# Decay products in one rounded form, one tile for a pair's turned exponentials, a sixth attention output, and another order of the work

## The chip, the cores and the metric

The kernel runs on one core of one Trainium2 chip. The metric is the time of one execution on the device in microseconds (us). A profile is one execution taken by the hardware profiler.

## The reference

Three stages on a batch of 4, 576 tokens, 8 heads of 64, all in float32:

```python
# 1. attention with a running decay, per batch and head
scores = scale * q @ k.T;  cum = cumsum(log(clip(f, 1e-4, 1)))
scores = where(causal, -1e9, scores + cum[:, None] - cum[None, :])
attn = exp(scores - max);  attn /= attn.sum() + 1e-9
x = attn @ v                                   # heads side by side: 576 x 512
# 2. gated feed-forward with a convolution over three tokens
h = relu(x @ w_in)                             # 512 -> 1024
x = (h * sigmoid(conv3(h, conv_w))) @ w_out    # 1024 -> 512
# 3. real part of a 2-D Fourier transform, layer norm, feed-forward
u = x + real(fft(fft(x, axis=tokens), axis=channels))
un = (u - mean(u)) / sqrt(var(u) + 1e-6)
out = u + relu(un @ w_ch1) @ w_ch2             # 512 -> 2048 -> 512
```

## The kernel before, in words

**Attention** goes by pairs of heads, 16 pairs. One tile `qk` holds q and k of both heads, one head in rows 0 to 63 and the other in rows 64 to 127. `score` makes the scores of a pair: for each block of 128 queries (`i` from 0 to 4) a product of q and k in fp32 over the keys up to the diagonal, and onto it, in the same PSUM bank, the decay, as a second product of a column that picks the head (`sel`) with rows that hold -8 times the running sum (`cum`). `cum` is float32 rounded to the form that the array takes in one pass (fp32r), so it is held in two parts, the rounded rows and what the rounding left, and a decay product has 64 rows: 0 to 63 for one head, 64 to 127 for the other. The blocks come as `TX`, block 4 in two halves with blocks 1 and 0, and `TY`, blocks 3 and 2; TX's ranges share banks, (4, first half) with 1 and (4, second half) with 0. There are `NS` = 4 banks for scores. VectorE adds the causal mask, keeps the minimum of each row (scores carry a minus sign) and writes to SBUF; ScalarE takes the exponential and its sum. `trans` turns the exponentials in blocks of 128 by TensorE, and `evac` copies them from PSUM into a tile `pt`, one for even and one for odd heads, on VectorE and ScalarE. `pv` multiplies with v for both heads, scales by the reciprocal sums into `xr`, and splits the result on ScalarE (rounded) and GpSimd (the rest) into a slot of `xs`, a ring of `NX` = 5.

**Pair 0** begins from nothing: `f` lands in `ft`, VectorE and ScalarE take the logarithm and the running sum in two halves and make `cum` from it. For the first of pair 0's groups of ranges (`SELF` = 1) the decay isn't taken from `cum`, but from `ft` itself in fp32, 32 rows, with a column of -8 in the head's row that comes behind f in the same tile. Its four products are issued together behind the four of q and k. Ahead of all that, `NWARM` = 4 matmuls of zeros, which nobody reads, occupy TensorE.

**The second stage**, for each batch of four pairs, is `bc_chunks`: eight chunks of x @ w_in (each matmul reads one slot of `xs`), the convolution and the gate, and then eight of the product with `w_out`. They are put between the steps of later pairs. The weights are unpacked from a 64-bit form by ScalarE, GpSimd and VectorE (`decode`). The third stage follows from about 380 us on: the transforms, and the last feed-forward.

**The order** is the kernel's own: operations are recorded in program order, and `Plan.order` places them by a list scheduler. `cost_of` gives the duration of each, `forward` places them on five queues, `backward` gives due times, both `ROUNDS` times over; a string of letters, `SHIFT`, then shifts each operation's due time. `lead` and `hold` make an operation due earlier, or keep it from a time before which it is not to start. What `together` records is emitted without anything between. Each engine then runs its queue in that order and waits for data by semaphores. Nearly all instructions thus have the line of two helpers: L596 for those recorded together, L607 for the others; they are told apart by their tiles: `att_qk` q and k, `att_t__67` and `att_t__66` `cum` and `sel`, `att_rb__68` `ft` at the start, `att_pt` the turned exponentials, `bc_xs` the attention outputs, `wprep` the weights on their way.

## Time and profile before

| | |
|---|---|
| median of 3 runs | 839.71 us (839.46 to 839.72) |
| the profiled execution's own time | 843.63 us |
| its span, first to last instruction | 841.9 us |
| TensorE busy | 820.2 us, 97% |
| VectorE, ScalarE, GpSimd busy | 640.0, 428.8, 243.8 us |

Busy times are sums over the whole span; the three stages have different fill. A fp32 matmul stands in the trace as two rows of one instruction each, a rounded one as one row; the ends of matmuls are modelled, so the distance from one start to the next says more than a row's own length. The column PEclk tells the clock that the throttle granted as a share of 2.4 GHz, where the profile recorded it.

### The profile page before, as it was taken

The page shows a single profiled execution, that of the slowest core. Times are in us where ns is not written, and L with a number is a line of the kernel's source. Part 1 is how long each engine was busy: PE and PEld are TensorE (multiplying, and loading weights), DVE is VectorE, ACT ScalarE, POOL GpSimd, SP SyncE. Part 2 cuts the span into 40 slices and gives each one's busy share as a digit, 9 for nine tenths or more (in the row PEclk, how much of TensorE's full clock was granted, in tenths as well). Part 3 has the DMA queues.
Part 4 walks back from the last instruction along what each step waited for, and adds up shares of the span by engine and source line. Part 5 has one row for each costly group of instructions (what it writes and reads, how often), then busy time and mean ns, then how long its engine had stood idle before and what let it go on. Part 6 is the DMA issues. An engine that isn't in the chain of part 4 may idle for free.

```text
span 841.9 us, 15293 instructions
## 1 busy us (share of the span) xinstructions
PE 820.2 (97%) x5392; PEld 706.0 (84%) x5392; DVE 640.0 (76%) x1598; ACT 428.8 (51%) x1053; POOL 243.8 (29%) x279
## 2 busy tenths in 40 slices
PE   9999999999999999998999999999999999999998
PEld 5667778699888988898888888888888889888886
DVE  6988899965996694159577979769778698967574
ACT  5987889843874673265344354335423452313120
POOL 1243445410361134177546460222012210000000
PEclk9999999999999999999999999999999999999999
DMA  6555456789248727785986844533646326241222
GB/s 203 170 163 168 152 177 213 221 290 284 105 132 258 245 83 231 256 259 164 251 240 161 195 145 121 168 114 93 207 142 160 125 76 187 52 151 38 80 72 87
DMA packets 98124, 139.67 MB, mean 166 GB/s; under 512 B 17076, under 2 KB 60116, under 8 KB 98048
## 3 DMA queue, kind: packets, MB, share of 16 engines
...
q0 software_dynamic: 576, 2.95, 1.1%
q8 instruction: 42, 0.69, 0.3%
q14 instruction: 34, 0.28, 0.1%
HBM read 105.78 MB, written 35.04 MB: 167 GB/s over the span
## 4 chain that ended last, share of the span: by engine, by line
PE 84%; DVE 7%; ACT 4%; DMA 2%; issue 1%; POOL 1%; SPq 0%; DVEq 0%; ACTq 0%; POOLq 0%
PE psc_c__4736 L607 11%; PE psc_c__4735 L607 11%; PE psbc_bc__549 L607 10%; PE psbc_bc__548 L607 10%; PE psdft_x__3965 L607 5%; PE psdft_x__3966 L607 5%; PE psatt_s__169 L596 4%; PE psc_c__4864 L607 4%; PE psc_c__4863 L607 4%; PE psc_c__4861 L607 4%; PE psc_c__4862 L607 4%; PE psatt_s__167 L596 3%; PE psatt_u__166 L607 2%; PE psatt_u__171 L596 2%; PE psatt_u__166 L596 2%; PE psatt_u__171 L607 2%
## 5 line engine op out<-in xcount | busy, mean ns | idle before, releaser
L607 ACT ACTIVATE bc_xs__131<-ml_t__5420 128x320 fp32r<-128x320 f32 (+1 forms) x78 | 34.9, 450 | 104.9 <-DVE ml_t__5420 L607 88.2
L607 PE MATMUL psbc_bc__548<-bc_xs__131,bc_wi__130 128*128 128x288 f32 x384 | 67.4, 303 | 1.1 <-ACT glu_t__138 L607 1.0
L607 PE MATMUL psbc_bc__549<-bc_xs__131,bc_wi__130 128*128 128x288 f32 x384 | 68.0, 304 | 0.1
L607 DVE TENSOR_TENSOR ml_t__5420<-psc_c__4736,ml_t__5420 128x320 f32<-128x320 f32 (+1 forms) x91 | 40.9, 462 | 23.6 <-PE psc_c__4736 L607 19.4
L607 DVE TENSOR_TENSOR ml_t__5420<-psc_c__4735,ml_t__5420 128x320 f32<-128x320 f32 (+1 forms) x91 | 40.9, 460 | 21.6 <-PE psc_c__4735 L607 20.0
L607 PEld LDWEIGHTS psbc_bc__548<-bc_xs__131,bc_wi__130 128*128 128x128 f32 x384 | 55.1, 188 | 2.6 <-ACT glu_t__138 L607 1.3
L607 PEld LDWEIGHTS psbc_bc__549<-bc_xs__131,bc_wi__130 128*128 128x128 f32 x384 | 55.2, 188 | 1.9 <-issue 0.7
L607 DVE SCALAR_TENSOR_TENSOR bc_xs__131<-ml_t__5420,bc_xs__131 128x320 fp32r<-128x320 f32 (+1 forms) x78 | 39.3, 508 | 15.0 <-ACT bc_xs__131 L607 13.5
L607 POOL TENSOR_SCALAR wprep_dw__125<-wprep_dw__125 128x512 f32<-128x512 f32 x24 | 16.4, 683 | 110.7 <-ACT wprep_dw__125 L607 110.7
L607 POOL TENSOR_SCALAR wprep_dw__122<-wprep_dw__122 128x512 f32<-128x512 f32 x24 | 16.6, 691 | 83.0 <-ACT wprep_dw__122 L607 83.0
L607 DVE SCALAR_TENSOR_TENSOR glu_cv__157<-glu_t__138,bc_cw__132,glu_cv__157 128x576 f32<-128x576 f32 x32 | 32.4, 1013 | 7.2 <-ACT glu_cv__157 L607 6.9
L607 DVE SCALAR_TENSOR_TENSOR glu_cv__158<-glu_t__139,bc_cw__132,glu_cv__158 128x576 f32<-128x576 f32 x32 | 31.4, 981 | 4.1 <-ACT glu_cv__158 L607 3.9
L607 DVE COPY glu_t__140<-psbc_bc__549 128x256 f32<-128x256 f32 (+2 forms) x48 | 9.9, 261 | 30.4 <-PE psbc_bc__549 L607 27.9
L607 ACT ACTIVATE ml_t__5422<-ml_t__5420 128x320 fp32r<-128x320 f32 (+1 forms) x26 | 11.5, 448 | 41.3 <-DVE ml_t__5420 L607 34.5
L607 ACT ACTIVATE glu_t__140<-psbc_bc__548 128x256 f32<-128x256 f32 (+2 forms) x48 | 8.6, 251 | 36.5 <-PE psbc_bc__548 L607 31.1
L596 PE MATMUL psatt_u__171<-att_pt__101,att_tv__92 128*64 128x448 f32 (+3 forms) x80 | 21.6, 417 | 1.0 <-ACT att_pt__102 L607 1.0
L596 PE MATMUL psatt_u__171<-att_pt__102,att_tv__93 128*64 128x448 f32 (+3 forms) x80 | 21.6, 417 | 0.0
L607 POOL TENSOR_TENSOR bc_xs__131<-att_xr__69,bc_xs__131 128x576 fp32r<-128x576 f32 x8 | 12.7, 1585 | 26.4 <-ACT bc_xs__131 L607 26.4
L607 ACT ACTIVATE wprep_dw__125<-wprep_dr__124 128x512 f32<-128x512 f32 x24 | 15.9, 663 | 8.6 <-DMA wprep_dr__124<-in_moe_w_ch_dram 4.1
L596 PE MATMUL psatt_u__166<-att_pt__102,att_tv__100 128*64 128x448 f32 (+4 forms) x72 | 19.3, 413 | 0.0
L596 PE MATMUL psatt_u__166<-att_pt__101,att_tv__99 128*64 128x448 f32 (+4 forms) x72 | 19.3, 413 | 0.0
L607 DVE SCALAR_TENSOR_TENSOR glu_cv__158<-glu_cv__158,glu_t__139 128x576 f32<-128x576 f32 x16 | 15.0, 936 | 4.9 <-ACT glu_cv__158 L607 4.9
(899 smaller groups left out, 2958.9 us busy)
## 6 DMA issues: line engine op xcount, KB each, us to landing
wprep_dr__124<-in_moe_w_ch_dram SPq DMA_DIRECT2D x16, 512.0 KB
...
bc_wo__133<-dram_t__328 SPq DMA_DIRECT2D x13, 512.0 KB
...
```

The lines of the kernel that those rows point to most:

```text
L596: getattr(eng[op.eng], f)(**{k: v.real() if isinstance(v, View) else v for k, v in kw.items()})
L607: getattr(eng[op.eng], op.fn)(**kw)
```

## The change

The decay products of all pairs take the rounded rows `cum`; the fp32 form, its column in the tile of f and the input that held it go. In pair 0 each range's products of q and k, and each range's decay products, are recorded as a group of their own; in the other pairs a group now has q-k and decay of one range before those of the next, and each range begins with a start flag of its own. The turned exponentials of a pair lie in one tile of 3840 columns instead of two of 2688: the odd head's blocks run backwards in the gaps of the even head's. The ring of attention outputs gets a sixth slot, in another pool. There are six warm-up matmuls instead of four. The later half of w_in may start at 20 us in the plan instead of 30, w_out at 50 instead of 60. The planner prices a group by its columns and the number of its matmuls, and its model of the clock has two levels of activity. `SHIFT` is another string, and there are 58 rounds instead of 27.

```diff
--- before.py
+++ after.py
@@ -21,14 +21,14 @@
 NZT, NZR, NPQ, NUN, NUS = 1, 1, 0, 2, 1
 NZS = 1
 G3 = 6
-NCV, NZZ, NZO, NX = 2, 4, 2, 5
-NUO, NWARM = 1, 4
+NCV, NZZ, NZO, NX = 2, 4, 2, 6
+NUO, NWARM = 1, 6
 LASTW = 256
 NTV = 4
-NPT = 1
-DRAIN = 120.0
-XW, H_IN, H_OUT, H_CH = 6, 3e4, 6e4, 0.0
-NS, NU, NSPLIT, SELF = 4, 2, 4, 1
+NPT, NXR, NRT = 1, 2, 2
+DRAIN = 200.0
+XW, H_IN0, H_IN, H_OUT, H_CH = 6, 0.0, 20000.0, 50000.0, 0.0
+NS, NU, NSPLIT = 4, 2, 4
 LINE = 64
 NPB = 2
 BK3 = (3,)
@@ -37,81 +37,81 @@
 NFO = DFF // 128
 NFC = DCH // 128
 HALF = S // 2
-ROUNDS = 27
+ROUNDS = 58
 LETTERS = "ABCDEFGHIJKLMNOPQRSTUVWXYZabcdefghijklmnopqrstuvwxyz0123456789+-"
 SHIFT = """
...
 """
 KW = [64 + 128 * i for i in range(5)]
-PTW, QW = 2688, S + 64
+QW = S + 64
 QK = QW + S
 UW, ZW = DM + 2, 640
 HL = ((0, 0), (1, 0), (0, 1))
@@ -293,7 +293,8 @@
 
 def cost_of(eng, fn, kw, subs=None):
     if subs:
-        return DRAIN + sum(cost_of(eng, f, k) for f, k in subs) / 2
+        one = [k["out"].free() / 2.4 * (2.0 if k["rhs"].dtype == F32 else 1.0) for _, k in subs]
+        return sum(one) + 10.0 * len(subs)
     o = kw["out"]
     src = kw.get("in_", kw.get("in0", kw.get("data0", o)))
     n = float(prod(o.shape[1:]))
@@ -505,14 +506,16 @@
 
     def forward(self, prio):
         ops, busy = self.ops, {}
-        wire, port = [0.0], [-1e9, -1e9]
+        wire, port, cold = [0.0], [-1e9, -1e9], [True]
 
         def place(i, t):
             o = ops[i]
             o.took = o.cost
             if o.eng == "PE":
                 tick = int(t // 3413.3)
-                if busy.get(tick - 1, 0) < 2500:
+                while len(cold) <= tick:
+                    cold.append(busy.get(len(cold) - 1, 0) < (3060 if cold[-1] else 2500))
+                if cold[tick]:
                     o.took = 2 * o.cost - 12.0
                 busy[tick] = busy.get(tick, 0) + o.work
             if o.pair:
@@ -701,8 +704,8 @@
             heads[2 * p + x] = dict(t=t[64 * x:64 * x + 64])
 
     plan.lead = 2 * LEAD
-    ft = att.tile([128, S + NH], F32, tag="rb")
-    one = att.tile([128, S], F32, tag="xr", bufs=2)
+    ft = att.tile([128, S], F32, tag="rb")
+    one = att.tile([128, S], F32, tag="xr", bufs=NXR)
     one, ft = one[0:NH], ft[0:NH]
     V.memset(out=one, value=1.0)
     dma(out=ft, in_=f)
@@ -725,7 +728,8 @@
     A.activation(out=sel, in_=mask[:, S:S + NH], func=AF.Copy)
 
     wi = bc.tile([128, 2, 4, DFF], F32R, tag="wi")
-    xs = bc.tile([128, NX, 2, S], F32R, tag="xs")
+    xs = bc.tile([128, 5, 2, S], F32R, tag="xs")
+    xs = [xs[:, i] for i in range(5)] + [ga.tile([128, 2, S], F32R) for _ in range(NX - 5)]
     cw = bc.tile([128, 3 * NFO], F32, tag="cw")
 
     def load_conv():
@@ -778,7 +782,9 @@
         Pt.append(row)
     sums = {}
     if NWARM:
+        plan.lead = 3 * LEAD
         V.memset(out=Pt[1][4][:, 0:256], value=0.0)
+        plan.lead = 0.0
         ps = ps_att.tile([128, 512], F32, tag="u", bufs=NU)
         for i in range(NWARM):
             mm(ps[:, 0:256], Pt[1][4][:, 0:128], Pt[1][4][:, 0:256], True, True)
@@ -794,42 +800,38 @@
     TX = (((4, 0, HALF), (1, 0, KW[1])), ((4, HALF, S), (0, 0, KW[0])))
     TY = (((3, 0, KW[3]),), ((2, 0, KW[2]),))
 
-    TXY = TX + TY
-
     def score(p, tiles):
         two = (2 * p, 2 * p + 1)
         if tiles[0] is TX[0]:
             sums[p] = att.tile([128, 2, 5], F32, tag="sum", bufs=2)
             for n in two:
                 heads[n]["nb"] = att.tile([128, 6], F32, tag="nb", bufs=4)
-        subs, picks, todo = [], [], []
+        subs, todo = [], []
         for items in tiles:
-            ps = [ps_att.tile([128, 512], F32, tag="s", bufs=NS) for _ in two]
-            col = 0
+            ps = None
             for i, c0, c1 in items:
                 w = KW[i]
-                if col and p == 0 and items is TX[0]:
-                    plan.together("PE", picks)
-                    ps, col, picks = [ps_att.tile([128, 512], F32, tag="s", bufs=NS) for _ in two], 0, []
+                if ps is None or p == 0 and items is TX[0]:
+                    ps, col = [ps_att.tile([128, 512], F32, tag="s", bufs=NS) for _ in two], 0
                 o = [z[:, col:col + c1 - c0] for z in ps]
                 for n in two:
                     t = heads[n]["t"]
                     subs.append(("matmul", dict(out=o[n % 2], lhsT=t[:, w - 64:w + 64], rhs=t[:, QW + c0:QW + c1],
-                                                start=col == 0, stop=False)))
+                                                start=True, stop=False)))
                 if p == 0:
                     plan.together("PE", subs)
                     subs = []
                 for n in two:
                     r = slice(64 * (n % 2), 64 * (n % 2) + 64)
-                    if p == 0 and items in TXY[:SELF]:
-                        one_of, row = ft[:, S + n:S + n + 1].over(0, [0, 128]), ft[:, c0:c1]
-                    else:
-                        one_of, row = sel[r].over(n, [0, 128]), cum[r, c0:c1]
-                    picks.append(("matmul", dict(out=o[n % 2], lhsT=one_of, rhs=row, start=False,
-                                                 stop=p == 0 and items is TX[0] or (i, c0, c1) == items[-1])))
+                    subs.append(("matmul", dict(out=o[n % 2], lhsT=sel[r].over(n, [0, 128]), rhs=cum[r, c0:c1],
+                                                start=False, stop=True)))
+                if p == 0:
+                    plan.together("PE", subs)
+                    subs = []
                 todo.append((i, c0, c1, o))
                 col += c1 - c0
-        plan.together("PE", subs + picks)
+        if subs:
+            plan.together("PE", subs)
         for i, c0, c1, o in sorted(todo, key=lambda x: (-x[0], x[1])):
             w = KW[i]
             for n in two:
@@ -848,17 +850,18 @@
         r = att.tile([128, 2, 5], F32, tag="r", bufs=2)
         V.tensor_scalar(out=r, in0=sums[p], scalar1=1e-9, scalar2=None, op0=ALU.add)
         V.reciprocal(out=r, in_=r)
-        rt = att.tile([10, 128], F32, tag="rt", bufs=2)
+        rt = att.tile([10, 128], F32, tag="rt", bufs=NRT)
         ps = ps_att.tile([128, 512], F32, tag="u", bufs=NU)
         transpose(ps[0:10, 0:128], r.over(0, [1, 10]))
         A.activation(out=rt, in_=ps[0:10, 0:128], func=AF.Copy)
         dma(out=Flat(r_d, 1280 * p, [128, 10], [1, 128]), in_=rt)
 
     def pt_hi(n, j, q, *dims):
-        return heads[n]["pt"].over(64 + 512 * j + q, *dims)
-
-    def evac(n, src, j, q, nb, step, eng):
-        h_ = pt_hi(n, j, q, [step, nb], [1, 128])
+        return heads[n]["pt"].over(3264 - 640 * j + q if n % 2 else 64 + 512 * j + q, *dims)
+
+    def evac(n, src, j, q, nb, eng, far=False):
+        step = (2560, -2048) if far else (512, -640)
+        h_ = pt_hi(n, j, q, [step[n % 2], nb], [1, 128])
         if eng is V:
             V.tensor_copy(out=h_, in_=src.group(nb))
         else:
@@ -866,7 +869,7 @@
 
     def trans(n, grp):
         if grp == 4:
-            heads[n]["pt"] = att.tile([128, PTW], F32, tag=f"pt{n % 2}", bufs=NPT)
+            heads[n]["pt"] = heads[n - 1]["pt"] if n % 2 else att.tile([128, 3840], F32, tag="pt", bufs=NPT)
         P = Pt[n % (2 * NPB)]
         ps = ps_att.tile([128, 512], F32, tag="u", bufs=NU)
 
@@ -879,32 +882,32 @@
 
         if grp == 4:
             full(4, 0)
-            evac(n, ps, 0, 448, 4, 512, V)
+            evac(n, ps, 0, 448, 4, V)
         elif grp == 3:
             full(3, 0)
             diag(3, 384)
-            evac(n, ps, 0, 320, 4, 512, A)
+            evac(n, ps, 0, 320, 4, A)
         elif grp == 2:
             full(2, 0)
             diag(2, 256)
-            evac(n, ps[:, 0:384], 0, 192, 3, 512, A)
+            evac(n, ps[:, 0:384], 0, 192, 3, A)
         else:
             full(1, 0)
             diag(1, 128)
             diag(0, 256)
             diag(4, 384)
-            evac(n, ps[:, 0:256], 0, 64, 2, 512, A)
-            evac(n, ps[:, 256:512], 0, -64, 2, 2560, V)
+            evac(n, ps[:, 0:256], 0, 64, 2, A)
+            evac(n, ps[:, 256:512], 0, -64, 2, V, True)
 
     xhl = {}
     xrb = {}
 
     def pv(p):
         two = (2 * p, 2 * p + 1)
-        rb = att.tile([128, S + NH], F32, tag="rb")
+        rb = att.tile([128, S], F32, tag="rb")
         for x in range(2):
-            dma(out=rb[64 * x:64 * x + 64, 0:S], in_=Flat(r_d, 1280 * p + 640 * x + 64, [0, 64], [1, S]))
-        xr = att.tile([128, S], F32, tag="xr", bufs=2)
+            dma(out=rb[64 * x:64 * x + 64], in_=Flat(r_d, 1280 * p + 640 * x + 64, [0, 64], [1, S]))
+        xr = att.tile([128, S], F32, tag="xr", bufs=NXR)
         subs, todo = [], []
         for q0, q1, js in ((128, S, (0, 2, 3, 4, 1)), (0, 128, (0,))):
             ps = ps_att.tile([128, 512], F32, tag="u", bufs=NU)
@@ -920,7 +923,7 @@
             V.tensor_tensor(out=xr[:, q0:q1], in0=ps[:, 0:q1 - q0], in1=rb[:, q0:q1], op=ALU.mult)
         for n in two:
             del heads[n]
-        xh, xl = xs[:, p % NX, 0], xs[:, p % NX, 1]
+        xh, xl = xs[p % NX][:, 0], xs[p % NX][:, 1]
         hi(xh, xr)
         lo(G, xl, xr, xh)
         xhl[p] = (xh, xl)
@@ -1013,7 +1016,7 @@
 
     prep = {}
     for k in range(8):
-        prep.setdefault(k // 2, []).append((load_w_in, 2 * k if k < 4 else 2 * k - 7, H_IN if k > 3 else 0.0))
+        prep.setdefault(k // 2, []).append((load_w_in, 2 * k if k < 4 else 2 * k - 7, H_IN if k > 3 else H_IN0))
         prep.setdefault(XW + k // 2, []).append((load_w_out, k, H_OUT))
     prep[0].append((lambda u: load_conv(), 0, 2e4))
     clear_pads()
@@ -1545,8 +1548,7 @@
         order += [b * S + t for t in [0] + list(range(257, 320))]
     c = lambda a: np.ascontiguousarray(a, dtype=np.float32)
     mask = np.concatenate([mask, np.tile(np.eye(NH), (4, 1))], axis=1)
-    pick = -8.0 * np.eye(NH)
-    return {"mask": c(mask), "pick": c(pick), "ident": c(np.eye(128)), "sgn": c(sgn), "dd": c(dd), "ds": c(ds)}, order
+    return {"mask": c(mask), "ident": c(np.eye(128)), "sgn": c(sgn), "dd": c(dd), "ds": c(ds)}, order
 
 
 def kernel(**inputs):
@@ -1568,7 +1570,7 @@
     data = [
         ("qk", qk),
         ("v", vp.reshape(B, H, 5, 128, D).transpose(0, 1, 3, 2, 4)),
-        ("f", np.concatenate([x["f"].reshape(NH, S), consts["pick"]], axis=1)),
+        ("f", x["f"].reshape(NH, S)),
         ("moe_w_in", bits(x["moe_w_in"])),
         ("moe_conv_w", bits(x["moe_conv_w"].reshape(3, NFO, 128).transpose(2, 1, 0).reshape(128, 3 * NFO))),
         ("moe_w_out", bits(x["moe_w_out"])),
```

## Rows read from the trace of the kernel before

**Rows 1.** The page: busy time, share of the span and instructions of each engine.
```profile
PE 820.2 (97%) x5392; PEld 706.0 (84%) x5392; DVE 640.0 (76%) x1598; ACT 428.8 (51%) x1053; POOL 243.8 (29%) x279
```

**Rows 2.** Windows: stretch and length in us, busy us per engine, clock, DMA, GB/s.
```profile
0.00:20.00 20.00, 17.93 (x69) 11.43 (x71) 12.35 (x45) 10.55 (x30) 2.51 (x25) 1.00 0.60 197
20.00:100.00 80.00, 74.04 (x594) 54.11 (x591) 69.23 (x235) 68.03 (x198) 31.60 (x30) 1.00 0.53 166
100.00:430.00 330.00, 321.14 (x2486) 287.08 (x2484) 240.37 (x571) 202.12 (x520) 131.93 (x128) 1.00 0.68 211
430.00:842.00 412.00, 407.06 (x2252) 353.43 (x2250) 318.02 (x751) 148.07 (x308) 77.80 (x97) 1.00 0.45 128
...
150.00:170.00 20.00, 18.08 (x143) 11.85 (x142) 17.96 (x60) 17.19 (x55) 7.16 (x6) 1.00 0.78 232
```

**Rows 3.** Timeline of TensorE, 4 to 19 us: start, length, instruction, idle before.
```profile
5.91 1.22 PE L607 MATMUL psatt_u__166<-att_t__80 128*128 128x256 f32 x2
...
7.41 0.69 PE L596 MATMUL psatt_s__169<-att_qk__70 64*128 64x192 f32 x1 [0.28 <-DMA att_qk__70<-in_qk_dram]
...
8.36 1.32 PE L596 MATMUL psatt_s__167<-att_rb__68 32*128 32x288 f32 x2
9.47 1.16 PE L596 MATMUL psatt_s__168<-att_rb__68 32*128 32x288 f32 x2
...
11.85 0.84 PE L596 MATMUL psatt_s__167<-att_qk__70 64*128 64x288 f32 x1
...
12.49 0.68 PE L596 MATMUL psatt_s__167<-att_qk__70 64*128 64x288 f32 x1
...
13.26 0.58 PE L596 MATMUL psatt_s__167<-att_t__67,att_t__66 64*128 64x288 f32 x1
13.26 0.58 PE L596 MATMUL psatt_s__168<-att_t__67,att_t__66 64*128 64x288 f32 x1
13.64 0.25 PE L596 MATMUL psatt_s__167<-att_t__67,att_t__66 64*128 64x64 f32 x1
...
18.40 0.40 PE L596 MATMUL psatt_s__169<-att_qk__91 64*128 64x288 f32 x1
```

**Rows 4.** Timeline of VectorE, 2 to 14 us.
```profile
4.77 0.91 DVE L607 SCALAR_TENSOR_TENSOR att_t__67<-att_rb__68,att_t__67 32x288 fp32r<-32x288 f32 x2 [0.51 <-ACT att_t__67 L607]
...
7.05 0.91 DVE L607 SCALAR_TENSOR_TENSOR att_t__67<-att_rb__68,att_t__67 32x288 fp32r<-32x288 f32 x2 [0.51 <-ACT att_t__67 L607]
10.68 0.46 DVE L607 CUSTOM_DVE_ANT_0 att_t__80<-psatt_s__168,att_t__65 128x288 f32<-128x288 f32 x1 [2.71 <-PE psatt_s__168 L596]
...
11.06 0.45 DVE L607 CUSTOM_DVE_ANT_0 att_t__75<-psatt_s__167,att_t__65 128x288 f32<-128x288 f32 x1
```

**Rows 5.** Timeline of TensorE, 21 to 27 us.
```profile
21.09 0.64 PE L596 MATMUL psatt_s__169<-att_qk__91 64*128 64x448 f32 x1
...
22.25 0.28 PE L607 MATMUL psatt_u__171<-const_t__61,att_r__97 128*10 128x128 f32 x1
...
23.47 0.53 PE L596 MATMUL psatt_s__167<-att_qk__91 64*128 64x320 f32 x1
...
25.38 0.44 PE L607 MATMUL psatt_u__171<-const_t__61,att_t__77 128*128 128x128 f32 x2
```

**Rows 6.** One tile each: copies from PSUM, ns min/median/max, starts, forms.
```profile
L607 DVE COPY att_pt__101<-psatt_u__166 x16: 408/551/694, 18.2 to 313.5; 128x512 f32<-128x512 f32 x8, 128x256 f32<-128x256 f32 x8
L607 DVE COPY glu_t__140<-psbc_bc__549 x48: 172/181/425, 171.8 to 430.6; 128x256 f32<-128x256 f32 x16, 128x31 f32<-128x31 f32 x16, 128x32 f32<-128x32 f32 x16
```

**Rows 7.** Timeline of TensorE at 108 us and of ScalarE at 133 us.
```profile
108.28 0.59 PE L596 MATMUL psatt_u__166<-att_pt__101,att_tv__99 128*64 128x448 f32 x1
...
133.42 0.67 ACT L607 ACTIVATE bc_xs__131<-att_xr__69 128x576 fp32r<-128x576 f32 x1
```

**Rows 8.** Groups by form, VectorE, 20 to 100 us: count, busy us, mean ns.
```profile
L607 DVE SCALAR_TENSOR_TENSOR wprep_dw__125<-wprep_dr__124,wprep_de__126 128x512 int32<-128x512 int32 x5 | 4.7, 938 | 0.1
L607 DVE SCALAR_TENSOR_TENSOR wprep_dw__125<-wprep_dr__124,wprep_dw__125 128x512 int32<-128x512 int32 x5 | 4.0, 810 | 0.0
```

More of the change, by code (lines that the diff above doesn't have):

```diff
@@ new lines @@
+BWiIKhTMJJLaBFBBBdLIDGIdLTDPv1+JBEDnHL-HC2Dzvw-HB+Dsh4lJBHIIBFB+BVYN9bponNkBBBBHCBKFBJFiBRYs2OalhIXBBfBBLj4BJK
+lEBB4MBENiBBBQfRBIuNIBBhfUFBGBEBEBCFEHpd4GboMT35UZYOu8zJ7W999+9-nz80z8BBNLFEFVRhVm7jlR--1-s+zT51c7gXTGBvTLrctq
+Jws--S-pBe0DFBBFJBJvYb6cM+031f99ga7nKHHQMV--jayyxCUbY9-+hDeK-LsKa7436vR-VmHjX--i7+-+808nakrWVMRO94-t9rec-6gBF-
+-B569-1dsno1gOR8+7-i950-Wd4wq8icVMcpcporh9IcQCsIrD9sf9-y0+92gKZDLNlnhfsSGmNNgpKdMdJJ-m--ug78NXH9nJne108XJtSNDB
+JBZBEFBDnCDa0tjGCBFCOVBBBTKBBCNOBTIIoiclDBD4KoMUifebHXaLVkrw+bBsz16869-7-jEgi----74-+6zwVv-ksNZng445-z91-+l8b-
@@ new lines @@
+-+85++6gk+sX5zwi4v4++steo9928Ywv+hgpnYIPURaGDLOIEnmKm99-5-m-99-+8tw1-1+tz97otourZ-XmdV7xGBFHUoXEBdFUvcS+-smjza
+pnXT21OhC17u136qwoGPSCCJBCbYCBLwOJdX7LfirinjZDTMm3euwZ1c9w59-267-r0ttK99GWUTWVWV0pBBo3Zf0i06ONXovSZ9x-s729-w7g
+-vFgtgxx33b763+995--xa757hfVWz227-z7lmRPOp4nuoq3-wFe--mDEI-b-oqjSkhVMO73oo-T40---Ltx1-p3OT3iBBY0n2taGEckprbuOc
+GGDEvNIIe71y4zvp2RbSlkq2z6fcYWaTBBBBoEBBGBMBBKHZBgSCISBKBZYRCBBBBBBBBBBbQEB8WBBBB53Hmb9sm1pBBab5BBrdWBHBkFiMHB
+BINaBBKXBHHVXOTXC5VKTDBIBDQBK7zo7rlU43--URCrUp28393lq1lp8QK-3QS+--9muNBBHuu0wBuIPIFOBgPBPQBBvEBBBFBlJEJLLBBBGJ
@@ new lines @@
+BBBHBFK7S-+++++9+9mm+9fkOEEXFLNESkDSX2JGGOQyPBLjjXYNJFJKIkgomIGKIegKBBBdVust01-085mQVpn--y3-YOETaRpUhbB-9ySbON
+JlizgQq-dgCJLBBFGFXP0WOY3oBSIQMONN-2zukktgWSzUSjlY67r+TtHHCP2EZd5RbQrNBBBNVDuBMsBDDDBj5jWJBBE7YBSoCr-pOfLBGGWf
+FOmPyLskHITRfcQPFYJltxbR0-gJwNaFHtxtFBHXGZEHJOc8Y00zV4WN-aiprOCbsVUrjfsOx---zBBTsbq3BBBggry3WmDHJL7iQyosj8H9hk
+jW2u11PFECHBBBBMldr-y-i+58svn8-82+425-73XfWfnp5r0p-+867Z-ZsO1QB3OJFJ9bbztoRmaBCBFsZZbmwQgXeUZ5--ply8-+m+iyBD8a
+-w2+KJFsHdcTTLaLGLeNXaHs3EbcYWuchkGocelewmKDmlGCCIEFCECCCCBBBBCBBBBBBIBBBBIutBBcbXsBNBBBBBBGBGBBBBBBBFBBBBBBBB
@@ new lines @@
+BBCBJSBBBDBBJDBOBBCBBBBBFBBBBBBBBBBBEDFNKHBKTr-wbcBIeOLSEEELBKHBFOCFGvIDkpBB6V--QGBG7IISXEEH0mNZOHcn+g113YefLC
+LDPDQFSEBDldRKOSTcgrZoMPmsps-tw8e-kGfazBUBMBIEGFnw3pKQ0TVOJebdt+4-+-2++97H--yZ6-FJ4a-88wgia09k9kn46B6myi9999wt
+063xsqwy+xMKCmMzCYXNHVWOedlSkdDHeaSdioSfqYSRgTLFBPBCNfsVGWEfnPQ-8-+p---jdU7yhv+--g4QD2G+KLLHKDJDDDNHORlGUBPEBR
+RRRWRR0BBpEEBPCaZN1CBEBYYBQLTWYWIpHo0IBBMO0Q-2FeBDP0BBBJKBDBCB6gdyNunr-BB2w+Qpc--------7prw--3--4---g7z-gv04kF
+2b2jHTURMIWpcBNVHRBehTdgiG8OIC-cgy698++-tCDJLcQPy052-ZZkRHGOVmoXrCBMiT4R5bEyT80JD3-RU28-qw8lrw-iecq0LJ46p+TBvU
@@ new lines @@
+XL2WPW7mNIFUKJ8nDCBvI8oTvlLGBMcltQBBXBQGS6MDEHBGFNETcGqiFBOKK-WHHGFeDUHKTcQDZJhRoDfeLMXGCHBMNLGeJCYENICNYEFHBN
+fTPCBU6RCLoYlqv1u507v0wnLYeIig6gd0o-uNhvrGR0sto9isu7DQOKKDECFgjzBBHBTQBRDEEHORqblhSgcqUOjNQurhg4NY-tixnUHIFFEB
+DEBGCRISXO+c-BB-98-7++-PTsHy-lyPZMhPDbOEFKJ7EBEEmLSdB7naHf4-y27a--66e9bXws0six06fn9p-4+-te9-+46x1w0645kz-6++z0
+RkoRFax+yyIB9x2r34zVp--8s-f4mq8uVDwVzf7n+-DJWQBChxZv3YLfsqRgLU+69gvmzKBJBRCCEtGINHGIBGPbjpZBVRPNRWdxoglipEBBh0
+fD5-8s2-tJkc9-7WQS616PxWL2ZBPBYBBBBBBfBBBBKNBBDJBBE03UrDZqzBCeL55551554--o-3---p-+u-+-998+9B04DSDk3MNxdZGYNRGX
@@ L112 @@
+7Y8ys8VyhUWBBBFckeBYVUTeefb9-Va6Y71+w7rvz0C42mn0067Ib-3750VlBlMOUdZhhFCRBo3d14+x9v6267OE9fGGgYwVv+-9V9--+---9-
++----8------99Q9+qo-m-9B7x70du+6B5QQ5-4y-8+--8-+-++---+--9+wbtlpRxrdiJXZCPVTT-249+--z172-g691+z4-86--6-089---2
+-459Z899-9---9--8---+z+7771877+mxk5+--wJfnuvyZpPFjnTW-d-VJmIZ-TPgYfeuLPhMQLLjNXqTp33-pSsn10X-d6ZZ1kx
 """
 KW = [64 + 128 * i for i in range(5)]
-PTW, QW = 2688, S + 64
+QW = S + 64
 QK = QW + S
```

110 lines of the change are left out of this document (41 added, 69 removed).

## The prediction

> **What bounds the kernel now.** I read the engine totals first: TensorE is busy 820.2 of the span's 841.9 us [rows 1], so at most 21.7 us of idle time can go there, plus whatever its matmuls lose by running slowly. Then the stages, because the average hides them [rows 2]. From 430 us on, TensorE is busy 407.06 of 412 us; the 4.9 us left lie mostly at the end, after the last matmul, and nothing in the change shortens that stage's arithmetic. From 100 to 430 us it idles 8.9 us of 330. From 20 to 100 us it idles 6.0 us of 80, with VectorE at 69.2 and ScalarE at 68.0: three engines nearly full on the chain products, minimum, exponential, turn, product with V. In the first 20 us it idles only 2.1 us, yet that is where most can go, because there the matmuls are slow. The third view is TensorE in order of time from 4 us [rows 3]: the same half of a 64x288 fp32 product takes 0.68 us at 12.49 and 0.40 us at 18.40. The windows print a granted clock of 1.00 for this stretch too; by the durations the level was 1.2 GHz at 12.49 and 2.4 GHz by 18.40. The fourth is VectorE beside it [rows 4]: it waits 2.71 us for the first finished range, until 10.68.
>
> **First step: rounded decay products for pair 0's first bank.** Before, these four products are exact fp32 from 32 rows, each standing as two rows of the trace, the two heads one after the other: they hold TensorE from 8.36 to 11.85, 3.49 us [rows 3]. Now they are the rounded form that all others have. There both heads start together, and a pair of 288 columns takes from 13.26 to 13.64, 0.38 us at the slow clock [rows 3]. Two such pairs are 0.76 us at most (the second has 192 columns), so TensorE saves 2.7 us. What ends later is checked against its inputs. The rounded rows' first half is complete when VectorE's two operations from 4.77 end, at 5.68 [rows 4]; the first range's q-k product is done by 5.91. So no new wait shows for range one. Range two still waits for its DMA until 7.41; its product ends at 8.36, its decay near 8.74 instead of 11.85. The third range needs the two banks of range one, and before it started at 11.85, behind VectorE's two minima from 10.68 (0.38 us apart, 0.45 us long). VectorE still has to make the second half of the rounded rows from 7.05 to 7.96; if the minima stand behind that, they end near 8.8, and range three starts at about 9.0: 2.8 us earlier. I take -2.7 us. Behind a wait for the rounded rows TensorE's queue would hold range two, which cannot start before 7.41 anyway; that is the cover, 1.7 us of it from 5.68. Bounds: -1.5 (the added warm-ups in the way, below) to -3.1.
>
> **Two more warm-up matmuls, and the clock.** One warm-up matmul is two rows, 1.22 us at 5.91 [rows 3]; two more are 2.4 us. Nobody reads their result, and before 7.41 TensorE has 1.2 us or so to spare, so up to 1.2 us stands in the way. What they may buy is an earlier rise of the clock. If the level rises at the same instant as before, the work that moved ahead by 2.8 us is done at half speed, a loss of up to 1.4 us. If it rises at 9 us, six microseconds of slow work halve, 2.9 us. The 32-row products that go lie just ahead of the late rise. I take -0.8, nearer to the middle, because VectorE's minima do not shrink with the clock. The Trainium skill (TensorE: Matmul & The Clock Gate, "What's actually happening") says that the clock is released by activity kept up over a stretch of time and not by a number of matmuls. By that rule alone two more matmuls buy nothing and this term would be 0, the sum 0.8 us smaller; the trace agrees so far that a TensorE occupied from 4 to 12 us was still slow at 12.49 [rows 3].
>
> **Ranges issued singly, flags set per range.** The later pairs' products come as q-k, q-k, decay, decay per range, instead of all q-k first. The trace holds one such sequence by accident: 320 columns with their decay, then 288 and 192, from 23.47 to 25.38, 1.91 us against 1.67 us of columns (five passes at 2.4 GHz), 0.24 over. A lone 448 chunk from 21.09 to 22.25 is 1.16 against 0.93, 0.23 over [rows 5]. So going from a decay product back to a q-k product costs 0.02 us at most. With four more such turns for each of 15 pairs this is 0 to 1.2 us; I take 0, as the row has it. The start flag adds no instruction.
>
> **One tile for a pair's turned exponentials.** Instructions, elements and the reader (one group of PV products for both heads) stay. The odd head's blocks run backwards. No row shows a copy that writes its blocks backwards; the nearest is VectorE's copy of 256 columns that reads PSUM backwards, 425 ns at most, against 408 for the shortest copy of 256 columns into the old tile [rows 6]. I take 0, with +0.02 us for each of the odd heads' 80 copies as the bound, 1.4 us on engines that are not the last in most stages. A wait of one head's copy on the other's could only show where both are late; one tile already took both engines' copies before.
>
> **The sixth attention output.** Pair 5's PV product starts at 108.28, but ScalarE rounds its output only at 133.42 [rows 7]: slot 0 of the ring of five is held by pair 0 until the last first-stage chunk of batch 0 has read it. Pairs 6 to 8 then bunch, and from 150 to 170 us TensorE idles 1.9 us with VectorE at 17.96 of 20 [rows 2]. A sixth slot lets pair 5 go before. The filler matmuls lie beside it either way; I take half of that idle time, -1.0, bounds 0 and -1.9.
>
> **Order, lead and hold values.** The smaller tile for f and the shorter rows of its DMA are nothing against a wait at 7.41. The new order itself cannot be priced; it can move idle time from 20 to 430 us, 14.8 us in all [rows 2], both ways.
>
> **Sum.** -2.7 - 0.8 - 1.0 = -4.5 us. The profiled execution took 843.63 us, so 839.1 like for like; the timed runs' median is 839.71, 0.5% less, which gives 835.2 us. The start's gain reaches the end if TensorE's later work keeps its length: 20 to 100 us is a chain of nearly full engines, and 430 to 842 us is full [rows 2].
>
> **Rivals.** One, the order also heals stalls: half of the 14.8 us goes, another 6.4 us beyond the 1.0 counted: 828.8. For it speaks that VectorE and ScalarE have slack from 100 us on [rows 2]; against it, that from 20 to 100 us they have hardly any.
> Two, the start is given back: VectorE at 69.2 of 80 us has 10.8 us of slack, and if the first four pairs are paced by it and not by their start, PV of pair 3 comes when it came: 839.7.
> Three, slower: weights earlier. The input weights' later half may now start at 20 us instead of 30, and the next weights at 50 instead of 60. One block costs VectorE two operations of 0.94 and 0.81 us in this stage [rows 8], 1.75 us. Four blocks put ahead of pair 3's minima delay everything that follows by up to 7.0 us, and TensorE has no other work before pair 3 is done. With the 3.5 us of the start, 843.2. It decides from two blocks moved (3.5 us). For it: VectorE is the second fullest engine there; against: a later due time may still put the blocks where they were.
> Four, the decay products do not run earlier because the rounded rows are ready later in the new order: TensorE then waits to about 9 us and the start gains under 1 us; it belongs with the second rival's time.
>
> **How the numbers follow.** Forecast, 835.2 (831.5 to 838): 0.38. Stalls healed, 828.8 (822 to 831.5): 0.25. Given back, 839.7: 0.14. Slower, 843.2 (841.4 to 850): 0.23. This kernel's measurement can tell 0.2%, 1.7 us. Faster is the first two, 0.63, same 0.14, slower 0.23. The range from 824 to 845.5 leaves out about 0.06 below and 0.08 above; it holds the -1.5 to -3.1 of the start, the clock's +1.4 to -2.9, the 1.2 us of the turns and the 1.4 us of the copies.
>
> **What would show it.** The first step is right if VectorE's first minimum starts near 8 us instead of 10.68 and range three near 9. The clock: the first 64x288 half of 0.40 us stands before 15 us. The sixth slot: pair 5's rounding follows its PV product by a few us, and TensorE idles less from 100 to 200 us. The third rival shows as more weight operations on VectorE before pair 3's PV product (71 us less the start's gain). Wrong altogether: TensorE's busy time from 430 us grows, or idle time from 20 to 430 us exceeds 18 us.

## The result, and the profile after

The changed kernel takes 846.23 us (median of 7 runs, 843.46 to 847.53) against 840.08 us for the kernel before (7 runs beside it): ratio 1.0059, 95% interval 1.0038 to 1.0080. By the ratio it is slower by some 5 us, where 4.5 us less were forecast. Its profiled execution took 846.23 us, a span of 844.4.

The page of the changed kernel, busy time of each engine, beside [rows 1]:

```profile
PE 818.1 (97%) x5392; PEld 704.8 (83%) x5392; DVE 633.6 (75%) x1598; ACT 432.5 (51%) x1053; POOL 243.8 (29%) x279
```

TensorE has 2.1 us less to do and the span is 2.5 us longer: 4.6 us more idle time. Its windows (columns as in [rows 2]) say where:

```profile
0.00:20.00 20.00, 15.73 (x97) 11.30 (x97) 16.20 (x67) 14.14 (x43) 3.12 (x26) 1.00 0.67 222
20.00:100.00 80.00, 74.21 (x594) 54.35 (x592) 72.00 (x235) 69.61 (x200) 34.55 (x32) 1.00 0.54 172
100.00:430.00 330.00, 320.54 (x2465) 287.92 (x2462) 232.84 (x550) 199.22 (x504) 127.80 (x124) 0.99 0.67 209
430.00:842.00 412.00, 407.61 (x2248) 351.27 (x2246) 312.56 (x748) 149.54 (x308) 78.28 (x97) 1.00 0.44 127
150.00:170.00 20.00, 16.05 (x116) 12.52 (x117) 14.95 (x46) 13.77 (x40) 7.53 (x7) 0.91 0.71 237
```

The start is lighter by 2.2 us. From 20 to 100 us TensorE is as busy as before, with VectorE at 72.0 instead of 69.2. The stretch from 150 to 170 us has lost 2.0 us of busy time, at a mean granted clock of 0.91.

The start itself went better than forecast (range three starts at 7.91 us; about 9 was forecast). TensorE, 0 to 13 us (columns as in [rows 3]):

```profile
1.19 4.65 PE L610 MATMUL psatt_u__114<-att_t__80 128*128 128x256 f32 x12 [1.19 <-DVE att_t__80 L608]
...
6.12 0.40 PE L599 MATMUL psatt_s__115<-att_qk__70 64*128 64x288 f32 x1
...
6.15 0.50 PE L599 MATMUL psatt_s__115<-att_t__67,att_t__66 64*128 64x288 f32 x1
...
7.39 0.43 PE L599 MATMUL psatt_s__117<-att_qk__70 64*128 64x192 f32 x1 [0.73 <-DMA att_qk__70<-in_qk_dram]
...
12.15 0.66 PE L610 MATMUL psatt_u__114<-const_t__61,att_t__75 128*128 128x128 f32 x4 [0.61 <-ACT att_t__75 L610]
```

The six warm-ups (12 rows) stand without a gap, the 64x288 half takes 0.40 us already at 6.12 (2.4 GHz), the first decay pair stands at 6.15, and the first transposes at 12.15. VectorE's first minimum, against 10.68 in [rows 4]:

```profile
6.69 0.46 DVE L610 CUSTOM_DVE_ANT_0 att_t__75<-psatt_s__115,att_t__65 128x288 f32<-128x288 f32 x1
```

The largest wait of TensorE after the start, and what runs behind it:

```profile
165.28 0.85 PE L610 MATMUL psbc_bc__547<-glu_t__155,bc_wo__143 128*128 128x288 f32 x2 [2.95 <-DMA bc_wo__143<-dram_t__329]
165.92 0.44 PE L610 MATMUL psbc_bc__547<-glu_t__163,bc_wo__143 128*128 128x288 f32 x1
```

TensorE stands 2.95 us for the second load of output weights, and then one 128x288 matmul takes 0.44 us; without that wait (x4 below) it takes 0.29. From 165.28 to 168.70 us the granted clock is 0.50. So the wait costs a second time, by the lower level of the clock. SyncE's queue around the load:

```profile
150.50 0.56 SPq L610 DMA_DIRECT2D dram_t__329<-wprep_dr__130  x1
...
156.92 0.33 SPq L610 DMA_DIRECT2D wprep_dr__130<-in_moe_w_ch_dram  x1
157.34 1.13 SPq L610 DMA_DIRECT2D att_rb__68<-dram_t__328  x2
158.52 0.58 SPq L610 DMA_DIRECT2D bc_wo__143<-dram_t__329  x1
```

The load reads what the store from 150.50 writes, is issued at 158.52, and TensorE wants it at 162.3. In the kernel before the same load is issued at about the same time (160.98, and 158.30 in its repeated execution, b2 below), but its first reader stands at 169.76 (166.93 in b2), behind PV of pair 9:

```profile
160.98 0.43 SPq L607 DMA_DIRECT2D bc_wo__134<-dram_t__328  x1
```
```profile
169.76 0.40 PE L607 MATMUL psbc_bc__549<-glu_t__145,bc_wo__134 128*128 128x288 f32 x1
```

So the load did not move back; the new order brought its reader forward. The next large waits stand at 400 and 439 us:

```profile
400.08 0.40 PE L610 MATMUL psbc_bc__546<-glu_t__158,bc_wo__143 128*128 128x288 f32 x1 [1.54 <-ACT glu_t__158 L610]
439.15 0.39 PE L610 MATMUL psdft_x__3961<-dft_t__3772,dft_t__3774 128*128 128x256 f32 x1 [1.68 <-ACT dft_t__3774 L610]
```

### The profile page after: what moved, and what is told of

It is laid out like the page before. It is cut to its first block, busy times and chain, and to the rows that moved or that the text cites. A ratio compares the mean times of both kernels' runs of the same rounds, so it can differ in the third digit from the quotient of the medians.

```text
span 844.4 us, 15271 instructions
## 1 busy us (share of the span) xinstructions
PE 818.1 (97%) x5392; PEld 704.8 (83%) x5392; DVE 633.6 (75%) x1598; ACT 432.5 (51%) x1053; POOL 243.8 (29%) x279
## 3 DMA queue, kind: packets, MB, share of 16 engines
q0 software_dynamic: 576, 2.95, 1.2%
## 4 chain that ended last, share of the span: by engine, by line
PE 53%; DVE 4%; POOL 2%; ACT 2%; issue 1%; SPq 1%; DMA 1%; DVEq 0%; POOLq 0%; ACTq 0%
PE psc_c__4741 L610 10%; PE psc_c__4740 L610 10%; PE psdft_x__3956 L610 5%; PE psdft_x__3955 L610 5%; PE psbc_bc__546 L610 4%; PE psbc_bc__547 L610 4%; PE psc_c__4876 L610 4%; PE psc_c__4875 L610 4%; PE psc_c__4874 L610 3%; PE psc_c__4873 L610 3%; DVE glu_cv__168 L610 1%; SPq L610 1%; POOL dft_t__3774 L610 1%; PE psdft_x__3961 L610 1%; PE psatt_u__119 L599 1%
## 5 line engine op out<-in xcount | busy, mean ns | idle before, releaser
L610 PE MATMUL psbc_bc__546<-bc_xs__140,bc_wi__139 128*128 128x288 f32 x336 | 63.3, 305 | 1.6 <-ACT glu_t__148 L610 1.6
L610 PE MATMUL psbc_bc__547<-bc_xs__140,bc_wi__139 128*128 128x288 f32 x336 | 63.3, 305 | 0.4 <-POOL bc_xs__140 L610 0.2
L610 PEld LDWEIGHTS psbc_bc__546<-bc_xs__140,bc_wi__139 128*128 128x128 f32 x336 | 49.7, 188 | 3.5 <-ACT glu_t__148 L610 2.4
L610 PEld LDWEIGHTS psbc_bc__547<-bc_xs__140,bc_wi__139 128*128 128x128 f32 x336 | 49.8, 188 | 2.0 <-POOL bc_xs__140 L610 0.8
L610 DVE SCALAR_TENSOR_TENSOR bc_xs__140<-ml_t__5425,bc_xs__140 128x320 fp32r<-128x320 f32 (+1 forms) x78 | 36.4, 470 | 12.2 <-ACT bc_xs__140 L610 11.7
L610 DVE SCALAR_TENSOR_TENSOR glu_cv__167<-glu_t__148,bc_cw__141,glu_cv__167 128x576 f32<-128x576 f32 x32 | 28.8, 899 | 10.7 <-ACT glu_cv__167 L610 10.5
L610 ACT ACTIVATE att_pt__101<-psatt_u__114 128x256 f32<-128x256 f32 (+2 forms) x48 | 23.3, 486 | 15.0 <-PE psatt_u__114 L610 14.6
L610 ACT ACTIVATE att_pt__101<-psatt_u__119 128x256 f32<-128x256 f32 (+2 forms) x48 | 23.3, 485 | 9.8 <-PE psatt_u__119 L610 7.1
L599 PE MATMUL psatt_s__118<-att_t__67,att_t__66 64*128 64x192 f32 (+2 forms) x47 | 25.1, 533 | 0.0
L599 PE MATMUL psatt_s__117<-att_t__67,att_t__66 64*128 64x192 f32 (+2 forms) x47 | 25.0, 532 | 0.0
L599 PE MATMUL psatt_s__115<-att_t__67,att_t__66 64*128 64x288 f32 (+2 forms) x49 | 21.2, 440 | 0.0
L599 PE MATMUL psatt_s__116<-att_t__67,att_t__66 64*128 64x288 f32 (+2 forms) x49 | 21.3, 441 | 0.0
```

The costliest lines, as they stand in the source:

```text
L599: getattr(eng[op.eng], f)(**{k: v.real() if isinstance(v, View) else v for k, v in kw.items()})
L610: getattr(eng[op.eng], op.fn)(**kw)
```

## The experiments

Two theories. **A:** the parts of the change are good or neutral, and the new order of the instructions costs the time. **B:** the parts cost it. To part them, an order was written out instruction by instruction in place of the planner's search. "Old" is the order of before, given to the changed kernel's instructions; "new" is the changed kernel's. A seam at T means: all that was planned before T in the one order, the rest in the other. The table makes the line numbers of these kernels larger by 45.

**Parts and order.**

```diff
-SHIFT = """..."""           # the search's letters
+SEQ = r"""..."""            # x1: old; x2: new to 24 us, then old; x3: old to 24 us, then new
...
     def order(self):
+        return ...           # the positions in SEQ
```

> The changed kernel with every part of the change (rounded decay products everywhere, first ranges issued singly, six warm-ups, one tile for a pair's turned exponentials, six attention outputs), but all its instructions written in the kernel before's order. Theory A, the parts are good and the new order loses their gain: faster than before by 2 to 5 us, 835 to 838. Rival B, the parts cost the time (interleaved q-k and decay products, both heads' copies in one tile): slower than before by 3 to 6 us, 843 to 846, like the changed kernel. Rival C, the parts and order are both nothing and the changed kernel's 5 us are its clock falls: 839 to 841 with one fall fewer.

Measured: 840.12 us, ratio to before 1.0000 (0.9988 to 1.0012). Rival B falls: all parts together cost no more than 1.0 us. But theory A's gain is not there either. Rival C's range holds this time too; x3 and the timed runs decide on it below.

> All parts of the change; the new order for the work planned for the first 24 us, the order of before from there on. Theory A: the start's gain of 5 us for the first transposes is kept at least by half, 834 to 837, and faster than the parts in the old order alone by up to 2 us. Rival B: 842 to 846. Rival D, the start's gain is given back whatever the order, since from 20 to 100 us VectorE and ScalarE pace the pairs: 839 to 841.

Measured: 840.34 us, 1.0001 (0.9991 to 1.0011). Neither A nor B: the time is D's. D's mechanism is not in the trace: against the repeated execution of the kernel before (b2, below) PV of pair 3 stands at 67.69 instead of 68.25 and that of pair 9 at 163.52 instead of 164.08, so the lead of 0.6 us outlasts the stretch from 20 to 100 us.

> All parts of the change; the order of before for the work planned for the first 24 us, the new order from there on. Theory A: the new order's later stretch has the loss, so this is no faster than the changed kernel, 845 to 849. Rival B (the parts cost it, the order is neutral): 843 to 847 too, so this run separates A from B only together with the old order's; if it is under 842, the new start itself was harmful.

Measured: 848.33 us, 1.0089 (1.0074 to 1.0105). The loss is made after 24 us, by the order. Falls of the clock alone (rival C) are not enough for it: of the changed kernel's 7 runs the one with the highest mean granted clock, 0.999, still took 843.46 us, and x15 below, whose profiled execution has no fall of the clock before its last 2 us, took 844.45 in it; the 29 runs of the kernel before beside x15 took 838.42 to 842.79.

**The late load.**

```diff
-            dma(out=wos[u], in_=wo_d[:, u // 2, 4 * (u % 2):4 * (u % 2) + 4])
+            half = 0 if b == 0 and u == 1 else u % 2
+            dma(out=wos[u], in_=wo_d[:, u // 2, 4 * half:4 * half + 4])
# x4: and this load stands directly behind the first one in the order
```

With this edit the product reads the first half of these weights twice and leaves the second out, so x4, and x6, x12 and x13 that share it, compute something else; they serve for the time alone.

> The changed kernel in its own order, but the second load of output weights of batch 0 (wanted by TensorE at 162.3 us, landed at 165.23 in the changed kernel) reads the first half of these weights in place of the second and is issued right behind the first load, some 45 us earlier. Theory A: the idle 2.95 us at 162 goes, and with it the clock's fall from 165.28 to 168.70, 1.7 us: 841.5 to 843.5, that is 3 to 4.7 us less than the changed kernel. Rival: the wait is only passed on to the next late item (pair 9's PV, the copies), 845 to 847.

Measured: 842.22 us, 1.0021 (1.0009 to 1.0033). The wait is gone, as theory A has it, and the ratio is lower than the changed kernel's by 0.0038, 3.2 us. Busy time of the kernel with the early load, and of the changed kernel, from 160 to 180 us:

```profile
160.00:180.00 20.00, 19.46 (x154) 16.16 (x155) 12.67 (x45) 11.05 (x33) 4.61 (x6) 1.00 0.92 297
```
```profile
160.00:180.00 20.00, 17.05 (x125) 14.07 (x125) 9.26 (x29) 7.92 (x26) 1.22 (x2) 0.91 0.77 249
```

2.4 us more busy time, and all of it at full clock (x10 below, which keeps the wait, has a mean of 0.83 in this window); the matmul that took 0.44 us:

```profile
164.50 0.29 PE L655 MATMUL psbc_bc__547<-glu_t__163,bc_wo__143 128*128 128x288 f32 x1
```

1.8 us over before are left.

**The kernel before once more, and its warm-ups.**

```diff
# b2: no change
-NUO, NWARM = 1, 4
+NUO, NWARM = 1, 6            # x7, order of before written out
```

> The kernel before, unchanged, profiled once more, because its first profile (843.63 us) lies above its median (840.42 over 29 runs) and all parts in the old order timed the same as before although their start stood 3 us ahead of that profile. Theory E: the first profile caught a late rise of the clock (matmuls at half speed to 17.8 us); a usual execution near 840 has full speed some 5 to 10 us earlier, and then its 64x288 half of 0.40 us stands before 13 us. Rival: the start is the same as in the first profile and the 3 us lie in later falls of the clock.

Measured: 839.48 us. Theory E holds, though its sign comes only roughly: the 64x288 half takes 0.46 us at 10.29, and 0.40 first at 15.43, behind a relapse of the clock. TensorE of this execution, and two windows of it:

```profile
7.78 0.75 PE L596 MATMUL psatt_s__167<-att_rb__68 32*128 32x288 f32 x2
...
8.85 0.48 PE L596 MATMUL psatt_s__169<-att_rb__68 32*128 32x192 f32 x2
...
9.95 0.51 PE L596 MATMUL psatt_s__167<-att_qk__70 64*128 64x288 f32 x1 [0.29 <-DVE att_nb__95 L607]
...
14.49 0.65 PE L607 MATMUL psatt_u__166<-const_t__61,att_t__75 128*128 128x128 f32 x4
```
```profile
7.10:10.50 3.40, 2.99 (x17) 2.15 (x18) 2.18 (x10) 1.25 (x3) 0.18 (x1) 1.00 0.98 360
10.50:13.90 3.40, 3.40 (x18) 2.08 (x16) 2.63 (x11) 2.00 (x7) 0.43 (x1) 0.50 0.55 212
```

The 32-row products that took 1.32 and 1.16 us in [rows 3] take 0.75 and 0.64 here. The clock is up from 7.1 us, falls to 0.50 from 10.50 to 13.90, and the first transposes stand at 14.49 instead of 17.19. The profile on which the prediction rested had caught a late rise.

> The kernel before in its own order with two more warm-up matmuls behind its four, nothing else. If the warm-ups alone bring the earlier rise of the clock that the changed kernel shows at 4.86 us and it counts to the end: 837 to 838.5. If usual executions of before have that rise already (theory E), or the gain is given back between 20 and 100 us: 839.5 to 841. If they only stand in the way: 841 to 842.

Measured: 839.06 us against 840.58, ratio 0.9983 (0.9969 to 0.9997): 1.4 us less. The warm-ups alone are a small gain, and this is the only version with its own data that beat the kernel before.

**The weights ahead of pair 3 (the prediction's third rival).**

```diff
-SEQ: weight operations of the first 100 us where the new order has them
+SEQ: the same ones where the old order has them, by count of VectorE's other operations   # x5, x6 (with the early load)
```

> The changed kernel; only the operations that prepare the weights in the first 100 us stand where the order of before has them (31 instead of 37 of VectorE's ahead of pair 3's output, 39 instead of 44 ahead of pair 4's). Theory A1: VectorE's weight operations cause the loss of 2.5 us between 40 and 70 us, so 843 to 844.5, that is 2 to 3 us under the changed kernel's 846.2. Rival: the loss there comes from the order of the transposes and their copies, and this stays at 845.5 to 847.

> Both: the weight operations of the first 100 us where the order of before has them, and the second load of output weights reading the first half and issued early (other data). Theory A1: the two gains add, 839 to 841, the time of before; what is left of the new order is then neutral. Rival: the 2.5 us of the early stretch are not the weights', 841.5 to 843, as with the early load alone (842.2).

Measured: 873.62 and 869.8 us, ratios 1.0392 and 1.0342. Both failed as experiments: shifting them among the other operations made waits of its own, above all this one of the first:

```profile
137.45 0.48 PE L655 MATMUL psatt_u__114<-const_t__61,att_t__74 128*128 128x128 f32 x1 [9.70 <-DVE att_pt__101 L655]
```

They say nothing on the weights' price.

**Where along the time the order loses.**

```diff
+SEQ: x9 new to 130 us, then old; x10 new to 385, then old; x11 old to 385, then new
+SEQ: x12 new to 385, then old, with x4's early load
```

> All parts of the change; the new order for the work planned for the first 130 us, the order of before from there on. Theory F, the new order loses at two places behind 130 us (the late load at 162 with the clock's fall, and the stretch from 400 to 480): 839 to 841, the time of before, although the first 70 us hold more weight work. Rival G, the early stretch with its additional weight work costs to the end: 842 to 843.5.

Measured: 842.75 us, 1.0029 (1.0016 to 1.0041). By the number G is right; but x12 below has, but for the early load, the same order to 130 us and is faster than before, so the early stretch cannot cost that by itself. The seam is the likelier cause; it was not shown.

> All parts; the new order for the work planned for the first 385 us, the order of before behind. Theory F: only the late load's price is left, 3 to 4.5 us over before, 843 to 845, that is 1.5 to 3 us under the changed kernel. Rival H, the whole loss is the late load and its clock fall, and the end is neutral: 845.5 to 847, as the changed kernel.

Measured: 844.62 us, 1.0041 (1.0027 to 1.0055): as F has it.

> All parts; the order of before for the work planned for the first 385 us, the new order behind. Theory F: the loss of the stretch from 400 to 480 alone, 1.5 to 3 us over before, 841.5 to 843.5. Rival H: 839.5 to 841.

Measured: 845.69 us, 1.0059 (1.0035 to 1.0082): the sign of F at twice its size. The trace shows both orders' waits, 2.28 us at 391 from the old one and 2.14 and 1.12 us at 403 and 441 from the new; the seam adds them up.

> The early second load (it reads the first half of the output weights of its group in place of the second) in the new order for the first 385 us, the order of before behind. Theory F: both losses gone, 839 to 841, 1.5 to 3 us under the early load alone (842.2). Rival G or H: 842 to 843.

Measured: 839.13 us, 0.9985 (0.9974 to 0.9996): as F has it. Windows from 420 to 480 us of the changed kernel, of x4, and of x12:

```profile
420.00:480.00 60.00, 57.64 (x330) 49.28 (x329) 44.94 (x104) 24.84 (x52) 29.34 (x44) 1.00 0.74 185
```
```profile
420.00:480.00 60.00, 57.94 (x322) 48.99 (x321) 46.91 (x109) 24.99 (x53) 30.50 (x45) 1.00 0.74 182
```
```profile
420.00:480.00 60.00, 59.92 (x335) 51.74 (x334) 50.19 (x113) 27.73 (x57) 34.07 (x49) 1.00 0.75 190
```

With the old order behind 385 us TensorE's 2.1 us of idle time there are gone. The wait on the tile of 400.08 is not: x12 stands 2.0 us for it, at 396.56. So what the old order mends lies behind 420 us.

**What in the last stretch, the queue's place, the decay products, a better version.**

```diff
# x13: x4, and two loads moved up
-SP: zt, zt, store, zz, zz, zt, zt, ..., store of glu_t__150
+SP: zt, zt, zt, zt, store, zz, zz, ..., store of glu_t__150
# x15: own data
-SP: store, tv, tv, wprep_dr, rb, rb, load of bc_wo__143
+SP: store, load of bc_wo__143, tv, tv, wprep_dr, rb, rb
# x8: kernel before, its order written out
-NS, NU, NSPLIT, SELF = 4, 2, 4, 1
+NS, NU, NSPLIT, SELF = 4, 2, 4, 0
# x14: changed kernel
+SEQ: old to 172 us, new to 385, then old
```

> The changed kernel with the early load of the half group (other data, as before), and with two of the four 256-KB loads of the first transform's rows, which the changed kernel issues at 428.11 and 428.61 us, moved up behind the first two (425.82). In the changed kernel the store issued at 431.74 behind them lands at 438.06, ScalarE writes over its buffer at 438.13 and TensorE stands 1.68 us to 439.15. Theory F1, that queue is the cause of the loss from 400 to 480: 839 to 840.5, against 842.2 with the early load alone. Rival: the store is late for another reason, the order of the work on ScalarE, and the time stays at 841.5 to 843.

Measured: 841.35 us, 1.0022 (1.0005 to 1.0039), against 1.0021 with the early load alone. F1 falls. The waits of TensorE from 420 to 480 us, first the changed kernel's, then x13's (total, times, longest):

```profile
PE psdft_x__3961 L610 <- ACT dft_t__3774 L610: 1.7, 1, 1.7
...
PE psc_c__4741 L610 <- ACT mr_t__4783 L610: 0.2, 1, 0.2
```
```profile
PE psc_c__4741 L655 <- ACT mr_t__4783 L655: 0.8, 1, 0.8
PE psdft_x__3955 L655 <- ACT dft_t__3774 L655: 0.6, 1, 0.6
```

In x4, which differs from x13 by the two loads alone, the wait on dft_t is 1.2 us and that on mr_t 0.3. So the wait on dft_t shrank and the one on mr_t grew; both end on ScalarE.

> The changed kernel with its own data; the second load of output weights of batch 0 is issued directly behind the store that it needs, ahead of three other transfers on SyncE's queue. The store lands at 156.87 and the load was issued at 158.52, so the load can start 1.6 us earlier of the 2.95 us that TensorE waits. Theory F: 844 to 845.5, 1 to 2 us less than the changed kernel; 842.5 if the clock's fall goes with it. Rival: the three transfers passed are wanted just as urgently, and the time stays at 846 or rises.

Measured: 845.79 us, 1.0066 (1.0051 to 1.0080): no gain, as the rival has it. The load passed five transfers, not three, and the queue stood for its store: it was issued at 157.48, only 1.0 us earlier, and the two loads of v behind it from 157.91 on instead of 152.88. The load's wait is gone, and TensorE stands a little later, for VectorE:

```profile
169.13 0.53 PE L655 MATMUL psbc_bc__547<-glu_t__151,bc_wo__142 128*128 128x288 f32 x2 [1.95 <-DVE glu_t__150 L655]
```

> The kernel before in its own order with one thing changed: pair 0's first bank takes the rounded decay products, as all other banks do. In its usual executions the four exact products take 1.9 us (7.78 to 9.66), not the 3.49 us of the first profile. The prediction's first step at that size: 838.5 to 840, 1 to 2 us less than before. Rival, the gain is absorbed by VectorE's and ScalarE's work between 20 and 60 us or by the hand-over at 388 us: 840 to 841.

Measured: 840.48 us, 1.0001 (0.9987 to 1.0014): the rival.

> All parts of the change; the order of before for the work planned for the first 172 us, the new order from there to 385 us, the order of before behind. Theory F: neither the late load nor the last stretch's loss, and the wait at 388 us of the old order goes: 837.5 to 839.5, faster than both kernels. Rival: the seams between the orders cost as much as at 130 us (1.7 us), 840 to 842.

Measured: 840.38 us, 1.0009 (0.9995 to 1.0023): the rival; its TensorE is busy 59.14 of the 60 us from 420 on; where it loses against x12 was not followed up.

## Why the prediction was wrong

**The start.** Its mechanism stands in the trace, the gain does not. The step that failed is the size: -2.7 and -0.8 were worked out from rows at 1.2 GHz, which the repeated execution of the kernel before has only in part. There the four exact products take 1.88 us (7.78 to 9.66), not 3.49, and range three starts at 9.95, not 11.85. In x1 the four rounded ones take 0.52 us (7.32 to 7.84), and range three starts where it was forecast, at about 9:

```profile
8.92 0.51 PE L644 MATMUL psatt_s__167<-att_qk__70 64*128 64x288 f32 x1 [1.08 <-DVE att_nb__95 L655]
```

That is 1.0 us earlier, not 2.8. The sum then took off the 3.9 us between profile and median in proportion, while 2.8 us of difference between the two profiles lie just where the change works: in the repeated execution the first transposes stand 2.7 us earlier and PV of pair 0 at 28.3 us instead of 31.1. The changed parts in the old order have it at 27.3, 1.0 us better, and in the new start at 27.7, although there the first transposes came at 12.55: TensorE waits 1.39 us at 19.31 for ScalarE. x8 has it at 28.8; its second range waited 1.20 us for a DMA.

Of x1's 1.0 us nothing is left in the time. It is still there at PV of pair 3 (67.24 against 68.25) and of pair 9 (163.08 against 164.08). So the second rival (0.14) has the time of x1 and x2, but not the mechanism: VectorE does not take the start back between 20 and 100 us. The wait that takes it up in the old order, in the repeated execution and in x1:

```profile
387.83 0.54 PE L607 MATMUL psbc_bc__548<-glu_t__141,bc_wo__133 128*128 128x288 f32 x2 [1.89 <-ACT glu_t__139 L607]
```
```profile
387.52 0.85 PE L655 MATMUL psbc_bc__550<-glu_t__141,bc_wo__132 128*128 128x288 f32 x2 [2.28 <-ACT glu_t__139 L655]
```

x1 comes earlier and waits longer. That is read from two traces, not shown by a run.

**The clock.** Two more warm-ups were worth 1.4 us by x7 (interval 0.3 to 2.6), against the 0.8 taken. By the rule of the Trainium skill (TensorE: Matmul & The Clock Gate, "What's actually happening"), read as I read it, the term was 0. But two more matmuls are also more activity without a break, and the rows agree with the rule in that sense: x7's trace has no relapse like that from 10.50 to 13.90 us in the repeated execution (x5's, x6's and x11's, with the same six, do have one before 20 us, so they make it rarer at most). The row that the prediction took for agreement, TensorE occupied from 4 to 12 us and still slow at 12.49, does not bear the rule out: the same program was fast from 7.1 us in the repeated execution. Nor does x7's trace show where its 1.4 us lie: its first transposes stand at 14.89 and PV of pair 0 at 28.56, not before the 14.49 and 28.29 of the repeated execution. Three of the 17 runs of the kernel before beside it took 842.85 to 845.02 us with a printed mean clock of 1.000, much like the profile with the late rise (0.999), and none of x7's 12 is above 842.01. That these three rose late is likely and not shown.

**Ranges singly, one pt tile.** 0 was taken; x1 bounds all parts together to 1.0 us either way, but does not part them. (80 copies at 0.02 us are 1.6 us, not 1.4; nothing hangs on it.)

**The sixth attention output.** Pair 5's PV stands at 99.1 us and its rounding, at last, close behind:

```profile
103.38 0.69 ACT L610 ACTIVATE glu_t__147<-att_xr__69 128x576 fp32r<-128x576 f32 x1
```

But the -1.0 for less idle time from 100 to 200 us failed: in the changed kernel TensorE idles more there, from 150 to 170 us 4.0 us instead of the 1.9 of [rows 2]. PV of pair 5 is some 6 us ahead of the repeated execution (105.4), that of pair 7 still 3.1 (133.4 against 136.5), but that of pair 8 stands at 149.9 against 149.1 and that of pair 9 only at 176.4 against 164.1: attention ran ahead, and then stood behind the product with the output weights instead of filling the time until they had come. That it is the slot which let it run ahead was not tried apart; in the old order, with the slot there, pair 5 is rounded at 129.6.

**The order, "cannot be priced".** This is the step that decided: the sum left the new order out as a term of nothing, and it cost 5 us. The bounds "both ways" for it held only idle time that was there, and neither the clock behind a new wait nor the stretch behind 430 us. The sign for "wrong altogether", idle time over 18 us from 20 to 430, did not come for that reason: it is 15.2 us in the changed kernel, against 14.8. The ratios split the 5 us: 3.2 for the late load with the clock behind it (x4), 3.0 for the stretch behind 385 us (x4 to x12), and -1.3 for the rest (x12). Worked out from the intervals, each is uncertain by 1 to 2 us. They are not quite additive: taken in the other sequence the stretch is 1.5 (x10), which is not clear of zero, and the load 4.7.

**The third rival (0.23, weights earlier)** had the sign, and its range (841.4 to 850) holds the time, but not the mechanism. VectorE does have 2.8 us more work from 20 to 100 us, and PV of pair 3 stands at 69.67 us against 68.25 in the repeated execution; but pair 4's stands at 84.6 against 86.2, so that loss is made good before 100 us. Direct proof failed with x5 and x6. What in the stretch from 420 to 480 us makes ScalarE late stays open; it is not the place of the two loads (x13).
